# A chunked recurrence with a gated FFN: one mask tile for all heads, decay factors by a small DMA, and a new order of all steps

## The chip, the cores and the metric

The kernel runs on one core of one Trainium2 chip. The metric is device microseconds of one execution of the whole kernel. Three runs of the kernel before gave 170.5, 170.62 and 171.06; the median is 170.62. Such a core has a matrix engine (PE, which writes to eight PSUM banks), a vector engine (DVE), an activation engine (ACT), a general engine (POOL) and a sequencer (SP) that here only issues DMAs. Each engine works through its own list of instructions in order; they meet through semaphores.

## The reference

```python
# r, k, v, w: (4, 8, 768, 48) f32; u: (8, 48)
for t in range(S):
    kt, vt, rt, wt = (k[:, :, t], v[:, :, t], r[:, :, t], w[:, :, t])
    cur = np.einsum('bhd,bhe->bhde', u[None] * kt, vt)
    y[:, :, t] = np.einsum('bhd,bhde->bhe', rt, state + cur)
    state = wt[:, :, :, None] * state + np.einsum('bhd,bhe->bhde', kt, vt)
...
x = y.transpose(0, 2, 1, 3).reshape(3072, 384)
a = x @ w1          # w1, w2: 384 x 1024
b = x @ w2
h = a * b @ w3      # w3: 1024 x 1024
return h @ w_out    # w_out: 1024 x 384
```

A recurrence over 768 time steps (4 batch rows, 8 heads, 48 channels a head) feeds a gated feed-forward block over 3072 tokens.

## The kernel before, in words

**Units.** Time is cut into six chunks of 128 steps. A unit (`UNITS`, L14) is one chunk of one or two batch rows: units 0 and 1 are chunk 0 of batch rows 0 and 1 alone, unit 2 is chunk 0 of rows 2 and 3, and units 3 to 12 are chunks 1 to 5, two batch rows each. `unit(t)` (L383) defines the recurrence of a unit, `block(t)` (L672) its feed-forward part, `loads(t)` (L310) its loads. The inputs are f32 in HBM; most loads go through POOL's queue, which converts them to bf16 on the way.

**Inside a unit.** `ln` takes the logarithm of w (L402). `cs` sums it along time by a matmul with the triangular matrix `LT` (L414), and, in every unit but those of the last chunk, adds one matmul with one column of ones for each pair of heads (L419): that gives the sum over the whole chunk with channels on partitions. `pc` (L426) takes its exponential, the factor by which the state decays over the chunk. `ne` and `e` (or `et`) take exponentials of the running sums with a minus or plus sign, and k and r are scaled by them (`KRk` L438, `KRr` L484 or `KRw` L468). Both are transposed, on PE (`trk`, `trr`, `trw`, with a copy back, `trke`, `trre`) or, in later units, by a DMA that SP issues (`dtr`, `dtk`). Units in `RAW` transpose r unscaled and get the running sum transposed by `csT` (L451). `m` (L549) multiplies the transposes to scores M[s, t]; scores with s >= t are set to zero, either by DVE in one multiply with `mask` out of PSUM (`msk`, L568) or, for those in `POOL_MASK`, by a copy on ACT (`mcp`, L555) and a multiply on DVE (L561) or a select on POOL (L563). `rk`, `ruk`, `dg`, `dv` (L518 to L537) give the diagonal term with u. `ys` multiplies with the state, `yi` (L594) the scores with v; `yb` (L612) adds the diagonal (for unit 1, in `Y_PE`, two matmuls `yd` at L603 and a copy do). y is transposed (`yt` and `xT`, or a DMA `dty`). `kv` (L647), `T` (L655), `S` (L663, with pc) and `Sb` (L668) carry the state on.

**Feed-forward.** w3 and w_out are multiplied once: `wt` transposes w3 (L365), `w3Te` copies it back, `wm` (L374) multiplies with w_out and `w34e` copies. wm_0 is the first of these eight products. Then `a` and `b` (L688) multiply with w1 and w2, `asb` copies a to SBUF on ACT (L693), `abT` multiplies it by b on DVE (L698), `o` (L704) multiplies with the product of w3 and w_out, `osb` copies (L709) and `st` stores (L714).

**Order.** Nothing is scheduled by a compiler. `ORDER` (L61) lists every step with its engine (`dv_8@POOL`); each engine's program is what the list gives it, in that order. `warm7@3` stands for three matmuls on zeros into bank 7 (L302), whose result nobody reads. `BANKS` (L38) gives each step its PSUM bank or buffer, so a step also waits for the one that used the bank before.

The change touches the constants, `LT`, `mask` and `u` at the start (L206 to L298), `cs` and `pc`, the two places that use the mask, and both lists.

Of the kernel before, what the change touches and what calls it, by code (L numbers as in the profile page):

```python
# [7 lines left out]
F32 = mybir.dt.float32  # L8
# [12 lines left out]
N_M = 4  # L21
N_PC = 4
N_X = 4
N_ASB = 3
# [4 lines left out]
RAW = {0, 1, 2, 3, 6}  # L29
N_PSUM = set()  # L30
DMA_R = {7, 8, 9, 10, 11, 12}
# [29 lines left out]
ORDER = """  # L61
table@ACT zeros@DVE u@SP win_0@POOL kin_0@SP rin_0@SP win_1@POOL vin_0@SP rin_1@POOL win_3@POOL kc_0@DVE padlw@DVE
padet@DVE ones@DVE kin_1@POOL mask1@DVE LT@POOL win_2@POOL ln_0@ACT rc_0@DVE rk_0@DVE warm0@18 cs_0@PE padr@DVE
kin_2@POOL padkr@DVE ln_1@ACT uc@ACT warm1@6 csT_1@PE w3_0@POOL pc_0@ACT cs_1@PE ruk_0@DVE et_1@ACT ne_0@ACT
vin_1@POOL pc_1@ACT I128@POOL mask@POOL warm3@9 trw_1@PE csT_0@PE trw_0@PE ln_3@ACT kin_3@POOL ne_1@ACT warm4@3
csT_3@PE KRk_1@DVE KRk_0@DVE rin_3@POOL rk_1@DVE warm6@2 trk_0@PE vc_0@DVE trk_1@PE KRw_1@DVE trke_0@ACT dg_0@DVE
rin_2@POOL et_0@ACT et_3@ACT KRw_0@DVE ruk_1@DVE w3_1@POOL warm7@8 m_0_0@PE trke_1@DVE ln_2@ACT cs_3@PE msk_0_0@DVE
wo@POOL kv_0@PE cs_2@PE vin_3@POOL m_1_0@PE pc_2@ACT ne_2@ACT msk_1_0@DVE warm4@2 wt_0_0@PE w3_2@POOL pc_3@ACT
wt_1_0@PE ne_3@ACT wt_0_1@PE dg_1@DVE vin_2@POOL kv_1@PE csT_2@PE S_0@DVE dv_0@DVE yi_1_0@PE et_2@ACT dv_1@DVE
win_4@POOL S_1@DVE warm7@3 yd_1@PE KRk_3@DVE ybc_1@ACT KRk_2@DVE warm7@2 trk_3@PE w3Te_0@ACT win_5@POOL Sb_0@DVE  # L70
yt_1@PE yi_0_0@PE wt_1_1@PE Sb_1@ACT yb_0@DVE trw_3@PE w3Te_1@ACT trke_3@DVE w1_1@POOL warm1@1 trw_2@PE KRw_3@DVE
trk_2@PE KRw_2@DVE warm4@1 m_3_1@PE rk_3@DVE warm7@1 m_3_0@PE trke_2@DVE mcp_3_0@ACT rin_4@POOL ruk_3@DVE warm7@4
m_2_0@PE wt_2_0@PE maff_3_0@DVE mcp_2_0@ACT ys_3@PE wt_2_1@PE msk_3_1@DVE xT_1@ACT maff_2_0@POOL warm0@1 wt_3_0@PE
warm1@1 wt_3_1@PE dg_3@DVE m_2_1@PE yt_0@PE mcp_2_1@ACT rk_2@DVE kin_4@POOL warm4@3 wm_0@PE ruk_2@DVE maff_2_1@POOL
yi_3_0@PE w3Te_2@DVE wm_1@PE w34e_0@DVE dv_3@POOL dg_2@DVE yi_3_1@PE w3Te_3@ACT wm_2@PE rin_5@POOL yb_3@DVE w34e_1@ACT
wt_4_0@PE xT_0@DVE wt_5_0@PE w2_1@POOL wt_4_1@PE w3Te_4@DVE warm0@1 yi_2_0@PE wm_3@PE kin_5@POOL w34e_2@DVE dv_2@DVE
wt_5_1@PE yi_2_1@PE ln_4@ACT w1_0@POOL w34e_3@DVE yt_3@PE wm_4@PE yb_2@DVE w3Te_5@ACT xT_3@DVE iw_4@ACT cs_4@PE
w2_0@POOL w34e_4@DVE wm_5@PE pc_4@ACT ln_5@ACT ne_4@ACT cs_5@PE w3_3@POOL a_0_1@PE e_4@ACT yt_2@PE pc_5@ACT iw_5@ACT
rw_4@DVE kv_2@PE vin_4@POOL a_3_2@PE ne_5@ACT xT_2@DVE KRr_4@DVE a_1_1@PE asb_0_1@ACT S_2@DVE win_6@POOL kv_3@PE
asb_1_1@ACT KRk_4@DVE trr_4@PE T_3@DVE e_5@ACT a_2_2@PE rw_5@DVE win_7@POOL trre_4@ACT a_2_3@PE KRr_5@DVE trk_4@PE  # L80
S_3@DVE w34e_5@ACT trr_5@PE asb_2_3@ACT rk_4@DVE vin_5@POOL b_2_2@PE Sb_3@ACT ruk_4@DVE trre_5@DVE b_2_3@PE b_1_1@PE
KRk_5@DVE rin_7@POOL b_3_2@PE abT_1_1@DVE b_0_1@PE dg_4@DVE asb_2_2@ACT trk_5@PE kin_6@POOL abT_0_1@DVE a_1_0@PE
trke_5@ACT abT_2_2@DVE a_0_0@PE abT_2_3@DVE asb_1_0@ACT a_3_0@PE rin_6@POOL asb_0_0@ACT trke_4@DVE a_2_1@PE
asb_3_2@ACT b_0_0@PE abT_3_2@DVE asb_2_1@ACT m_4_0@PE abT_0_0@DVE m_4_1@PE mcp_4_0@ACT a_3_3@PE msk_4_1@DVE wt_6_0@PE
Sb_2@ACT b_1_0@PE asb_3_0@ACT maff_4_0@DVE wt_6_1@PE ys_4@PE abT_1_0@DVE dv_4@POOL m_5_0@PE yi_4_0@PE msk_5_0@DVE
b_2_1@PE asb_3_3@ACT wt_7_0@PE ln_6@ACT win_8@POOL yi_4_1@PE a_3_1@PE yb_4@DVE wt_7_1@PE win_9@POOL b_3_0@PE rk_5@DVE
w3Te_7@ACT cs_6@PE abT_2_1@DVE ln_7@ACT kin_7@POOL b_3_1@PE w3Te_6@DVE a_2_0@PE ruk_5@DVE iw_7@ACT abT_3_0@DVE wm_7@PE
pc_6@ACT asb_3_1@ACT dg_5@DVE ne_6@ACT abT_3_1@DVE csT_6@PE dv_5@POOL asb_2_0@ACT yt_4@PE et_6@ACT cs_7@PE xT_4@DVE
kv_4@PE rw_7@DVE rin_8@POOL pc_7@ACT kv_5@PE ne_7@ACT a_4_3@PE T_5@DVE rk_6@DVE wm_6@PE e_7@ACT kin_8@POOL KRk_6@DVE
asb_4_3@ACT T_4@DVE win_10@POOL KRr_7@DVE ys_5@PE m_5_1@PE ln_8@ACT S_4@DVE b_4_0@PE msk_5_1@DVE vin_6@POOL w34e_7@ACT  # L90
yi_5_0@PE trw_6@PE iw_8@ACT b_4_3@PE w34e_6@DVE vin_7@POOL Sb_4@ACT trk_6@PE KRw_6@DVE ln_9@ACT yi_5_1@PE abT_4_3@DVE
b_2_0@PE rin_10@POOL yb_5@DVE a_4_0@PE win_11@POOL cs_8@PE trke_6@DVE asb_4_0@ACT b_3_3@PE pc_8@ACT iw_9@ACT
abT_4_0@DVE vin_9@POOL a_4_2@PE KRk_7@DVE ne_8@ACT a_4_1@PE abT_3_3@DVE S_5@POOL e_8@ACT abT_2_0@DVE o_0_0@PE
ruk_6@DVE asb_4_2@ACT kin_9@POOL rk_7@DVE asb_4_1@ACT m_6_0@PE rw_8@DVE ln_10@ACT ys_6@PE rin_9@POOL m_6_1@PE
KRr_8@DVE o_2_0@PE mcp_6_1@ACT msk_6_0@DVE iw_10@ACT cs_9@PE dg_6@DVE yt_5@PE pc_9@ACT yi_6_0@PE xT_5@ACT o_3_0@PE
maff_6_1@DVE ruk_7@DVE ne_9@ACT osb_0_0@DVE yi_6_1@PE osb_2_0@ACT b_5_1@PE dv_6@DVE st_0_0@SP e_9@ACT st_2_0@SP
b_4_1@PE dtr_7@SP Sb_5@ACT yb_6@DVE a_5_1@PE ln_11@ACT a_5_2@PE dg_7@DVE dtr_8@SP asb_5_1@ACT yt_6@PE rk_8@DVE
# [36 lines left out]
def kernel(  # L134
# [629 lines left out]
```

## Time and profile before

| | us |
|---|---|
| three runs, median | 170.62 |
| the profiled execution | 171.16 |
| its span, first to last instruction | 169.4 |
| PE busy (1998 matmuls) | 162.6 |
| DVE busy (221 instructions) | 134.1 |
| ACT busy (151) | 89.5 |
| POOL busy (83) | 86.2 |

The profiled execution is 1.76 us longer than its span; that is what lies around it. Busy times are of engines that work side by side. A busy PE is not a PE that does useful work: matmuls on zeros count too. The chain of waits follows the work that ended last back to the start and names, at each step, what it stood on.

### The profile page before, as it was taken

The numbers are of one execution on the slowest core, as the hardware profiler recorded it, in microseconds if no ns is written. First come the engines' busy times: TensorE is split into PE (matmuls) and PEld (weight loads), VectorE is DVE, ScalarE is ACT, GpSimd is POOL, SyncE is SP. The second block draws the span as 40 slices with busy tenths as digits, with TensorE's granted clock in tenths as the row PEclk, the third lists the DMA queues.
The fourth block names the chain that finished last, engine by engine and source line by source line (L and its number), as shares of the span: only waits on it lengthen the run. The fifth ranks groups of instructions, "written<-read, shape, count | busy, mean of one in ns | idle before, by whom it ended". The sixth has DMA issues, their size and how long they took to land.

```text
span 169.4 us, 4733 instructions
## 1 busy us (share of the span) xinstructions
PE 162.6 (96%) x1998; PEld 122.0 (72%) x1998; DVE 134.1 (79%) x221; ACT 89.5 (53%) x151; POOL 86.2 (51%) x83
## 2 busy tenths in 40 slices
PE   7999999999999999999999999999999799999991
PEld 2455765676999887876878787676888587686860
DVE  0568889786789999999999999997799867556260
ACT  3166575258947789689855986611632042330511
POOL 7899874894773838994049607294072023000000
PEclk9999999999999999999999999999999999999999
DMA  3999999999999999999959999959949944603313
GB/s 80 212 205 182 146 198 189 206 215 153 183 203 217 175 173 167 172 149 174 194 106 90 174 203 236 164 49 109 135 109 141 157 87 109 165 4 95 137 58 130
DMA packets 98837, 25.63 MB, mean 151 GB/s; under 512 B 90880, under 2 KB 96640, under 8 KB 98816
## 3 DMA queue, kind: packets, MB, share of 16 engines
q0 software_dynamic: 76320, 15.96, 104.3%
q1 hardware_dynamic: 22496, 9.38, 27.3%
q8 instruction: 15, 0.25, 0.6%
q14 instruction: 6, 0.05, 0.1%
HBM read 27.98 MB, written 4.72 MB: 193 GB/s over the span
## 4 chain that ended last, share of the span: by engine, by line
PE 73%; DVE 11%; DMA 7%; ACT 4%; issue 2%; POOL 1%; SPq 0%; DVEq 0%; ACTq 0%
PE banks L688 28%; PE banks L704 13%; PE banks L302 10%; PE banks L374 6%; DMA vin<-in_v_dram 5%; PE banks L549 3%; DVE abT L698 3%; PE banks L594 2%; PE banks L414 2%; PE banks L510 2%; PE banks L365 1%; DMA out_dram<-osb 1%; DVE dg L528 1%; ACT a_sb L693 1%; PE banks L647 1%
## 5 line engine op out<-in xcount | busy, mean ns | idle before, releaser
L688 PE MATMUL banks<-xT,w_bf 128*128 128x256 bf16 (+1 forms) x624 | 69.7, 264 | 0.5 <-DMA xT<-yb 0.4
L688 PEld LDWEIGHTS <-w_bf 128*128 128x128 bf16 x624 | 55.2, 98 | 7.8 <-issue 1.0
L693 ACT COPY a_sb<-banks 128x512 f32<-128x512 f32 x48 | 27.4, 594 | 27.8 <-PE banks L688 22.5
L698 DVE TENSOR_TENSOR abT<-a_sb,banks 128x512 bf16<-128x512 f32 x48 | 31.6, 681 | 10.4 <-PE banks L688 6.9
L704 PE MATMUL banks<-w,abT 128*128 128x384 bf16 x192 | 34.5, 326 | 0.1
L704 PEld LDWEIGHTS <-abT 128*128 128x128 bf16 x192 | 18.1, 98 | 10.7
L568 DVE TENSOR_TENSOR Mbf<-banks,mask 128x1024 bf16<-128x1024 f32 x17 | 20.4, 1219 | 1.6 <-PE banks L549 1.3
L302 PE MATMUL banks<-zeros 128*128 128x512 bf16 x66 | 19.9, 431 | 1.4 <-DVE zeros L243 1.3
L537 POOL TENSOR_TENSOR dv<-vin,dg 128x768 bf16<-128x768 bf16 x9 | 13.3, 1482 | 15.5 <-DMA vin<-in_v_dram 8.7
L709 ACT COPY osb<-banks 128x384 f32<-128x384 f32 x13 | 6.3, 482 | 21.7 <-PE banks L704 9.2
L329 POOL DMA_DIRECT2D win<-in_w_dram x13 | 15.0, 1157 | 1.1 <-POOLq L748 0.8
L329 POOL DMA_DIRECT2D rin<-in_r_dram x12 | 13.8, 1152 | 2.8 <-DMA w_bf<-in_moe_w_dram 2.5
L402 ACT ACTIVATE lw<-win 128x768 bf16<-128x768 f32 (+1 forms) x13 | 10.5, 811 | 8.7 <-DMA win<-in_w_dram 8.7
L329 POOL DMA_DIRECT2D vin<-in_v_dram x12 | 13.9, 1160 | 2.3 <-DMA w_bf<-in_moe_w_dram 0.9
L329 POOL DMA_DIRECT2D kin<-in_k_dram x12 | 13.8, 1153 | 1.7 <-issue 0.7
L612 DVE TENSOR_TENSOR yb<-banks,dv 128x768 bf16<-128x768 f32 (+1 forms) x12 | 11.1, 921 | 4.4 <-issue 1.8
L302 PEld LDWEIGHTS <-zeros 128*128 128x128 bf16 x66 | 6.5, 108 | 8.2 <-issue 3.8
L433 ACT ACTIVATE NEt<-banks 128x768 bf16<-128x768 f32 (+1 forms) x13 | 9.9, 765 | 3.6 <-PE banks L414 3.6
L663 POOL TENSOR_TENSOR Sst<-Tst,pc 128x384 f32<-128x384 f32 x4 | 3.7, 934 | 15.7 <-DVE Tst L655 15.6
L374 PE MATMUL banks<-wo_bf,w3T 128*128 128x384 bf16 x64 | 11.7, 325 | 0.0
L528 DVE TENSOR_REDUCE dg<-ruk 128x16 f32<-128x768 bf16 (+1 forms) x13 | 11.5, 881 | 0.0
L594 PEld LDWEIGHTS <-Mbf 128*128 128x128 bf16 x192 | 7.8, 96 | 2.5 <-issue 1.1
(83 smaller groups left out, 222.5 us busy)
## 6 DMA issues: line engine op xcount, KB each, us to landing
out_dram<-osb SPq DMA_DIRECT2D x24, 192.0 KB, 2.1
win<-in_w_dram POOLq DMA_DIRECT2D x11, 384.0 KB, 9.8
kin<-in_k_dram POOLq DMA_DIRECT2D x11, 192.0 KB, 7.8
rin<-in_r_dram POOLq DMA_DIRECT2D x11, 192.0 KB, 8.4
vin<-in_v_dram POOLq DMA_DIRECT2D x11, 192.0 KB, 8.7
w_bf<-in_moe_w_dram POOLq DMA_DIRECT2D x4, 512.0 KB, 11.6
w_bf<-in_moe_w_dram POOLq DMA_DIRECT2D x4, 384.0 KB, 12.3
wo_bf<-in_moe_w_out_dram POOLq DMA_DIRECT2D x1, 768.0 KB, 13.5
```

Source lines behind the costliest of these rows:

```text
L302: nc.tensor.matmul(banks[:, at, :], lhsT=zeros[:, :C], rhs=zeros, start=True, stop=True)
L329: QUEUE[eng].dma_start(dst, src)
L374: nc.tensor.matmul(one(f"wm{fi}")[:, :DM], lhsT=w3T[fi % 2][:, gi, :], rhs=wo_bf[:, gi, :], start=(gi == 0), stop=(gi == FI - 1))
L528: nc.vector.reduce_sum(dgs, ruks, axis=AX.X)
L537: e.tensor_mul(dvs, vv, dgs[:, :, None].to_broadcast([C, bh, D]))
L568: nc.vector.tensor_mul(Mbf[bank[f"M{t}_{b}"]], mview(), mask.rearrange("s (j q) t -> s j q t", j=2))
L594: nc.tensor.matmul(o[:, h % 2, b, h // 2, :], lhsT=M[:, h % 2, h // 2, :], rhs=vv[:, b * H + h, :], start=(not c and b == 0 and h < 2), st ...
L612: nc.vector.tensor_add(ybs.rearrange("t b (q e d) -> t e (b q) d", e=2, d=D), yview().rearrange("t e (x d) -> t e x d", d=D), dvs.rearrang ...
L688: nc.tensor.matmul(o[:, f, :], lhsT=wt[:, di, fi * P:(fi + 1) * P], rhs=x[:, di, :T], start=(di == 0), stop=(di == DI - 1))
L693: copier(eng)(a_sb[bank[f"sa{t}_{g}"]], one(f"a{t}_{g}"))
L698: nc.vector.tensor_mul(ab[:, g * per:(g + 1) * per, :T], sa.rearrange("p (f t) -> p f t", t=T), one(f"b{t}_{g}").rearrange("p (f t) -> p f ...
L704: nc.tensor.matmul(one(f"o{t}_{b}")[:, :DM], lhsT=ab[:, fi, b * C:(b + 1) * C], rhs=w34[:, fi, :], start=(fi == 0), stop=(fi == FI - 1))
```

## The change

- `mask` is one 128x128 tile, made on DVE as LT minus the identity, and is read again for each head. Before it was 128 x 8 x 128, a memset on DVE and a select on POOL.
- For units 6 to 10 (`ROW_PC`) the one-column matmuls go. `px` (ACT) takes the exponential of the last 32 rows of the running sum, for each batch row, into a row buffer `prow` (one buffer); `pd` (SP) sends the last row, 4 KB, to the 128 partitions of `pc`. For the other units the one-column matmuls are a step of their own, `cc`, apart from `cs`.
- u is loaded as one row of 384 numbers and spread to all partitions by a matmul with the first row of LT (`ub`) and a copy (`ue`). Before, the DMA wrote it to 128 partitions.
- `u_f` and the f32 landing places of unit 0's k, r and v share memory with the last two `abT` buffers. `Mbf` has 5 buffers for 4, `a_sb` 4 for 3.
- Unit 0 is no longer in `RAW`, unit 1 no longer in `Y_PE`; `POOL_MASK` is another set.
- `ORDER` and `BANKS` are new throughout. The 66 matmuls on zeros become 30. The first loads are issued by SP (w of unit 0, u, k), ACT (w of unit 1, r and v of unit 0) and POOL (the rest). 46 steps change their engine, most of them from DVE to ACT. vin_12 stands ahead of S_9 on POOL, vin_11 behind S_10; before, both stood behind S_9 and ahead of S_10.

```diff
-N_M = 4
+N_M = 5
-N_ASB = 3
+N_ASB = 4
-RAW = {0, 1, 2, 3, 6}
+RAW = {1, 2, 3, 6}
+ROW_PC = {6, 7, 8, 9, 10}
-POOL_MASK = {(2, 0), (2, 1), (3, 0), (4, 0), (6, 1), (7, 1), (8, 1)}
-Y_PE = {1}
+POOL_MASK = {(1, 0), (2, 0), (2, 1), (4, 1), (5, 0), (6, 1), (7, 1), (9, 1)}
+Y_PE = set()
...
+    prow = many(1, [P, P * NB * HP], F32, "prow")
...
-    mask = sb.tile([C, 2 * HP, C], BF, name="mask")
+    mask = sb.tile([C, C], BF, name="mask")
...
-        nc.gpsimd.affine_select(mask, mask, compare_op=Alu.is_gt, fill=0.0, base=0, channel_multiplier=-1,
-                                pattern=[[0, 2 * HP], [1, C]])
+        nc.vector.tensor_sub(mask, LT, I128)
...
-        nc.sync.dma_start(u_f, u.rearrange("h d -> (h d)").partition_broadcast(C))
+        QUEUE[eng].dma_start(u_f, u.rearrange("h d -> (h d)").rearrange("(p x) -> p x", p=1))
...
+        nc.tensor.matmul(one("ub")[:, :DM], lhsT=LT[0:1, :], rhs=u_r, start=True, stop=True)
...
-            if state:
+        if state and t not in ROW_PC:
+            @op(f"cc_{t}")
+            def _(eng):
                 o = col_view()
...
+        if state and t in ROW_PC:
+            @op(f"px_{t}")
+            def _(eng):
+                dst = own(prow)[96:].rearrange("t (e d b q) -> t b q e d", e=2, b=nb, q=HP)
+                for b in range(nb):
+                    nc.scalar.activation(dst[:, b, :, :, :D], cs_view()[96:, b].rearrange("t (q e d) -> t q e d", e=2, d=D),
+                                         Act.Exp)
+            @op(f"pd_{t}")
+            def _(eng):
+                QUEUE[eng].dma_start(PC, own(prow)[C - 1:C])
...
-                        nc.vector.tensor_mul(x, x, mask)
+                        nc.vector.tensor_mul(x, x, mask[:, None, :].to_broadcast([C, 2 * HP, C]))
...
-                    nc.vector.tensor_mul(Mbf[bank[f"M{t}_{b}"]], mview(), mask.rearrange("s (j q) t -> s j q t", j=2))
+                    nc.vector.tensor_mul(Mbf[bank[f"M{t}_{b}"]], mview(),
+                                         mask[:, None, None, :].to_broadcast([C, 2, HP, C]))
```

More of the change, by code (lines that the diff above doesn't have):

```diff
@@ L63 @@
[L63 to L92, printed above, removed]
@@ L128 @@
-asb_12_1@ACT o_11_0@PE abT_12_1@DVE o_12_1@PE osb_11_0@DVE st_11_0@SP st_9_0@SP o_12_0@PE osb_12_1@DVE st_12_1@SP
-osb_12_0@ACT st_12_0@SP
+zeros@DVE win_1@ACT win_0@SP padlw@DVE ones@DVE rin_0@ACT u@SP LT@POOL table@ACT kin_0@SP padr@POOL vin_0@ACT
+kin_1@POOL win_3@POOL ln_0@ACT ln_1@ACT warm0@8 cs_0@PE rin_1@POOL uc@ACT e_0@ACT cc_0@PE kc_0@DVE cs_1@PE win_2@POOL
+ne_0@ACT iw_0@ACT padet@DVE rc_0@DVE cc_1@PE csT_1@PE pc_1@ACT ub@PE pc_0@ACT I128@POOL KRk_0@DVE ue@ACT vin_1@POOL
+padkr@DVE ne_1@ACT rw_0@DVE vc_0@ACT warm4@4 trk_0@PE KRr_0@DVE w3_0@POOL padpx@DVE trr_0@PE KRk_1@DVE mask@DVE
```

206 lines of the change are left out of this document (124 added, 82 removed).

## The prediction

> **What bounds the kernel now.** I read the page first, then the chain of waits in order of time, then the busy time by stage.
>
> ```profile
> span 169.4 us, 4733 instructions
> PE 162.6 (96%) x1998; PEld 122.0 (72%) x1998; DVE 134.1 (79%) x221; ACT 89.5 (53%) x151; POOL 86.2 (51%) x83
> DMA  3999999999999999999959999959949944603313
> ```
>
> PE is busy 96% of the span, and the DMA engines are full (nine tenths or more) in nearly every slice up to 100 us. But "busy" does not mean useful here. The chain shows what PE was doing:
>
> ```profile
> 1.26 6.93 PE banks L302 x18
> 8.52 1.32 PE banks L302 x6
> ...
> 17.40 0.18 PE banks L419 x8
> ...
> 30.48 0.65 PE banks L302 x3
> 31.13 1.30 PE banks L374 x8
> ...
> 36.10 0.22 PE banks L302
> ...
> 161.77 3.91 PE banks L704 x24
> ```
>
> L302 is the warm-up matmul on zeros: filler that computes nothing. There are 66 of them, 65 ahead of 31.13 us, where the first product of w3 and w_out (wm_0, L374) starts. After it there is one, at 36.10. So the kernel has two parts with different limits. Ahead of wm_0, PE is not the bound: it fills its waits. From wm_0 on, PE runs real work to 161.77 + 3.91 = 165.68, and after that only a copy and a store are left (169.4 - 165.68 = 3.7 us of tail).
>
> ```profile
> core 0: us, PE busy (x) PEld busy (x) DVE busy (x) ACT busy (x) POOL busy (x), PEclk, DMA share, GB/s
> 8.00:31.00 23.00, 22.77 (x287) 14.46 (x286) 19.27 (x41) 14.54 (x26) 18.62 (x20) 1.00 1.73 186
> 31.00:42.00 11.00, 11.00 (x122) 7.51 (x121) 7.85 (x14) 5.76 (x10) 8.49 (x9) 1.00 1.79 190
> 42.00:92.00 50.00, 50.00 (x748) 42.48 (x745) 47.23 (x77) 38.44 (x66) 31.78 (x28) 1.00 1.80 168
> 92.00:134.00 42.00, 41.81 (x545) 31.71 (x544) 38.96 (x58) 19.65 (x34) 18.25 (x16) 1.00 1.29 150
> 134.00:165.70 31.70, 30.33 (x292) 23.34 (x289) 18.42 (x27) 8.86 (x16) 2.95 (x2) 1.00 0.38 96
> ```
>
> From 31 us on PE is idle only 42.00 - 41.81 = 0.19 and 31.70 - 30.33 = 1.37, together 1.56 us. DVE is nearly full from 42 to 92 (47.23 of 50), so the chain passes through it there, but PE does not starve. What sets the start of wm_0 is a load:
>
> ```profile
> 16.72 0.94 POOL L348 DMA_DIRECT2D wo_bf<-in_moe_w_out_dram  x1
> wo_bf<-in_moe_w_out_dram POOLq DMA_DIRECT2D x1, 768.0 KB, 13.5
> u_f<-in_u_dram SPq DMA_DIRECT2D x1, 192.0 KB, 3.8
> ```
>
> w_out is issued at 16.72 and lands 13.5 us later, at 30.2. The other loads stand ahead of it in full DMA engines. So the time is: start of wm_0, plus PE's work after it, plus PE's idle time, plus the tail: 31.13 + (134.55 - 1.56 = 132.99) + 1.56 + 3.7 = 169.4.
>
> **The change part by part: the start of wm_0.** I compared the two orders. The same loads stand ahead of w_out in both (w, k, r of units 0 to 3, v of units 0 and 1, two quarters of w3), so its landing moves by bytes. u goes from 192 KB spread over 128 partitions to one row of 1.5 KB. At the stage's 186 GB/s the 195,000 bytes saved are 1.05 us: landing at about 29.15. The first loads now leave from SP, ACT and POOL at once instead of SP and POOL. The first DMA slice (4.2 us) is only three tenths busy, so an earlier flow could give up to about 0.9 us more, and I keep 28.3 as the lower end. The Trainium skill ("DMA: Bandwidth & Descriptors", section "Issuing engines are not separate DMA queues") says that starting DMAs from several engines saves only the issuing time; by it the landing would stay at 29.15, and the sum goes by that anyway.
>
> PE's own steps ahead of wm_0 are the same set in both orders but for unit 0: csT_0, trw_0, yd_1 go; trr_0 and the u matmul come. What DVE does there:
>
> ```profile
> L285 DVE MEMSET mask<- 128x1024 bf16 x1 | 0.9, 912 | 0.2 <-issue 0.2
> L514 DVE COPY KRT<-banks 128x1024 bf16<-128x1024 bf16 x4 | 2.7, 683 | 0.0
> L568 DVE TENSOR_TENSOR Mbf<-banks,mask 128x1024 bf16<-128x1024 f32 x17 | 20.4, 1219 | 1.6 <-PE banks L549 1.3
> L561 DVE TENSOR_TENSOR Mbf<-Mbf,mask 128x1024 bf16<-128x1024 bf16 x4 | 2.8, 704 | 0.1
> ```
>
> DVE loses the mask memset (0.91), two copies of transposes (2 x 0.68, to ACT) and a masked eviction (1.22, to ACT and POOL); it gets an eviction at 1.22 for a multiply at 0.70, and one multiply (0.70) that POOL did. yb_1, one w3T copy and unit 0's two new products stand against v's conversion, KRw_0 and padr, about even. In all some 2 us less, beside 19.27 of 23 us now, so I take the landing as the limit. In before, three warm-ups (0.65 us) stand directly ahead of wm_0 and it starts 0.9 after the landing; in the new order one stands there. So 29.15 + 0.4 = 29.55: **1.6 us earlier**. Bounds: 28.3, and 31.1 if DVE and ACT get through units 0 to 3 no sooner than now.
>
> **PE's work after wm_0.** The steps are again the same set. Out go the one-column matmuls of units 6 to 10, five groups of eight at 0.18 = **0.9 us**, and the warm-up at 36.10, **0.2 us**. Changes between 64-row and 128-row matmuls are as many as before (31). Left: 131.9.
>
> **What replaces the columns.** Each pc activation becomes two px activations of 384 elements on 32 partitions, and a 4 KB DMA that turns one partition's row into 128 partitions of 8 numbers. No row shows either. For px the ends are the pc row and the 384-element row; I take the upper, as the elements per partition are the same: 0.96 for 0.18, five times, 3.9 us more on ACT. For the DMA the ends are 2.6 (the fastest SP transfer) and 6.9 (an SP load behind two others at the full start); I take 3, as SP holds nothing else then.
>
> ```profile
> L426 ACT ACTIVATE pc<-banks 128x8 f32<-128x8 f32 x9 | 1.6, 180 | 1.7 <-PE banks L419 1.7
> L433 ACT ACTIVATE NEt<-banks 128x384 bf16<-128x384 f32 x2 | 1.0, 480 | 0.0
> wide_r<-in_r_dram SPq DMA_DIRECT2D x1, 192.0 KB, 6.9
> xT<-yb SPq DMA_TRANSPOSE x10, 2.6
> L709 ACT COPY osb<-banks 128x384 f32<-128x384 f32 x13 | 6.3, 482 | 21.7 <-PE banks L704 9.2
> L514 ACT COPY KRT<-banks 128x1024 bf16<-128x1024 bf16 x2 | 2.0, 1012 | 1.9 <-PE banks L510 1.9
> L693 ACT COPY a_sb<-banks 128x512 f32<-128x512 f32 x48 | 27.4, 594 | 27.8 <-PE banks L688 22.5
> ```
>
> The result is wanted late: between px_6 and S_6 PE has 25 us of work by these rates. The stretch of the order that PE now runs from 42 to 92 gives ACT 72 steps for 65: beside px three more osb (1.4), two more KRT copies (2.0), one more copy of scores, of the same size (1.0) and one more a_sb (0.6); the rest evens out. ACT gets 38.4 + 9 = 47.4 of 50 us. DVE has 76 steps for 78. Both fit, barely; ACT's cover is thin.
>
> **The mask** as one tile read again for each head: the nearest rows are ruk, which reads u again for each batch row, and rk, which reads nothing twice:
>
> ```profile
> L522 DVE TENSOR_TENSOR ruk<-rk,u_bc 128x768 bf16<-128x768 bf16 x11 | 6.1, 557 | 0.1
> L518 DVE TENSOR_TENSOR rk<-rin,kin 128x768 bf16<-128x768 bf16 x11 | 6.0, 549 | 0.0
> ```
>
> 8 ns apart: I count nothing. The other end would be the four SBUF multiplies at 1219 for 704, 2 us on DVE.
>
> **PE's idle time.** Of the 1.56 us, 0.9 is one wait:
>
> ```profile
> PE banks L594 <- DMA vin<-in_v_dram: 0.9, 1, 0.9
> 126.31 8.74 DMA vin<-in_v_dram
> 135.09 0.36 PE banks L594 x8
> ```
>
> POOL issues vin_12 and vin_11 behind S_9 (and vin_11 just ahead of S_10), and yi_11_0 wants vin_11 at once. In the new order vin_12 comes ahead of S_9, and between vin_11 and yi_11_0 PE has about 17 us of work, twice the 8.74: this wait goes. What is late next is unknown: every order was found anew, so I take 0.7 us of new idle, nearest to the 0.66 that the old order has beside vin. Net **0.2 us** less. Ends: no new idle, and the slower rival.
>
> **Sum:** 1.6 + 0.9 + 0.2 + 0.2 = 2.9 us off the span, 166.5. The profiled execution took 171.16 (span 169.4 and 1.76 around it), 0.54 over the median of 170.62; from the median, 167.7.
>
> **The rivals.** (1) *The start is not set by w_out.* If units 0 to 3 pass DVE and ACT no earlier, wm_0 stays at 31.1 and 1.3 us are left: 169.3. For it: DVE is 84% busy there. Against it: the load is later than all but one of these steps now.
>
> (2) *Slower: ACT waits for the small DMA.* prow is one buffer, so px of a unit waits until the DMA of the unit before has landed, and ACT's later steps (a_sb, which frees PE's banks) queue behind it. px_6, 7, 8 and 9 stand 4.6 to 4.9 us of PE work apart; less 0.96 for px, it costs from a landing of 3.7 us on. With 6.9, three waits of 3.2 = 9.6 us, at about 54 to 69 us, where the DMA row shows nine tenths; ACT's free 2.6 us of the stage take some, 7 us reach PE: 174.7. Against it: 4 KB on an otherwise empty SP queue.
>
> (3) *A cold array.* The first 18 warm-ups took 6.93 us, 0.385 each, the next six 0.22: PE starts at half rate. With 30 warm-ups for 66, PE ahead of wm_0 has long holes. If it is at half rate when wm_0 starts, the steps that end the prologue (some 1.5 us) double and wm starts slow for about as long as at the start (the early excess, 18 x (0.385 - 0.22) = 3 us): 4.5 in all, cut to about 3 because some of it hides behind w_out's landing: 170.7, no change. The Trainium skill ("TensorE: Matmul & The Clock Gate", section "Part 1: The HAM clock gate") says that the array falls back to half rate after an idle window of about 3.4 us; the two rates are in these rows, the falling back in none. Against it: the holes are broken by warm-ups and by units 0 to 3.
>
> (4) *The change doesn't do what it says*: the columns hide behind something. From 31 us PE is never idle for long, so this holds only where DVE sets the pace (73 to 92 us); units 8 and 9 then give nothing, 0.4 us: inside the forecast.
>
> **How the numbers follow.** Forecast 0.54, its own range 165.8 (wm_0 at 28.3, no new idle) to 169.0; rival 1 0.17; rival 2 0.18; rival 3 0.08; more gain than the bounds 0.03. A measurement of this kernel tells about 0.3% (0.5 us) from no change. Faster: 0.54 + 0.17 + 0.03, less 0.03 for rival 1 with more new idle time, is 0.71. Same: that 0.03 and 0.06 of rival 3, 0.09. Slower: rival 2 and the worse 0.02 of rival 3, 0.20. The range leaves out the lowest case and the upper half of rival 2: 165.3 to 171.8.
>
> **What would show it.** wm_0's first matmul at 29 to 30 us, right behind w_out's landing (rival 1: well behind it). No one-column matmuls for units 6 to 10, and PE's work from wm_0 to its last matmul near 131.9 plus idle. No wait of PE on vin. ACT's px near 0.48 each; the DMA's landing near 3 us, and no ACT wait on it (rival 2: a row of px waiting for that DMA). Warm-ups and transposes at half rate past 20 us would be rival 3. The forecast is wrong if PE's idle time after wm_0 exceeds 4 us, or w_out lands after 31.

## The result, and the profile after

| | before | changed |
|---|---|---|
| median of the runs of this comparison, us | 170.84 (4 runs) | 185.91 (4 runs) |
| the profiled execution | 171.16 | 184.54 |
| its span | 169.4 | 182.8 |

The ratio is 1.085, interval [1.077, 1.093]: the changed kernel is 8.5% slower; the forecast was 1.7% faster. Throughout, executions more than 1.5% above the fastest of their kernel do not enter the ratio (one of these four), the times given for e7, e9, e10, e16 and e17 are means of the executions that do, and the traces of e7, e16 and e17, which are of such long executions, are not read.

One correction to the section on the change: 48 steps change their engine, not 46, and 22 of them go from DVE to ACT.

The head of the page of the changed kernel; the DMA row is in 40 slices, 4.57 us each:

```profile
span 182.8 us, 4620 instructions
PE 160.6 (88%) x1917; PEld 119.4 (65%) x1917; DVE 127.9 (70%) x208; ACT 108.5 (59%) x186; POOL 84.1 (46%) x83
DMA  6999999999999999990069699977979901261213
```

PE is busy 88% of the span for 96%, ACT 108.5 us for 89.5. The first DMA slice is six tenths full for three. Around 82 to 91 us the DMA engines are empty, and then they fill again: the late loads come in a bunch. PE's instructions, in order of time, with the idle time ahead of them in brackets and what ended it (the first row, and those with the long waits):

```profile
27.80 2.44 PE L391 MATMUL banks<-wo_bf,w3T 128*128 128x384 bf16 x14
...
67.48 0.48 PE L434 MATMUL banks<-lw,LT 128*128 128x384 bf16 x2 [2.02 <-ACT lw L422]
...
80.52 1.91 PE L739 MATMUL banks<-w,abT 128*128 128x384 bf16 x7 [3.24 <-ACT NEt L467]
...
113.07 0.40 PE L583 MATMUL banks<-KRT 64*128 64x128 bf16 x8 [2.55 <-DMA KRT<-KR]
...
121.17 0.82 PE L723 MATMUL banks<-xT,w_bf 128*128 128x256 bf16 x6 [1.02 <-DVE yb L647]
...
129.22 1.47 PE L723 MATMUL banks<-xT,w_bf 128*128 128x256 bf16 x12 [2.14 <-DVE abT L733]
...
131.69 0.81 PE L723 MATMUL banks<-xT,w_bf 128*128 128x256 bf16 x6 [1.00 <-DMA xT<-yb]
```

wm_0 starts at 27.80. In the same view of the kernel before it starts at 30.97 (the 31.13 of the prediction is from the chain):

```profile
30.97 1.46 PE L374 MATMUL banks<-wo_bf,w3T 128*128 128x384 bf16 x8
```

So it comes 3.2 us earlier. The front gained, and more than forecast. The loss lies behind it, in two places. The busy time by stage, first of the changed kernel, then of the kernel before, shows both:

```profile
56.00:86.00 30.00, 22.68 (x300) 16.59 (x299) 22.59 (x33) 22.87 (x34) 16.17 (x14) 0.94 1.73 126
86.00:104.00 18.00, 17.90 (x216) 14.01 (x214) 16.11 (x28) 15.28 (x25) 8.09 (x6) 1.00 0.63 100
104.00:134.00 30.00, 23.24 (x337) 17.43 (x335) 19.62 (x31) 16.61 (x38) 12.14 (x11) 1.00 1.73 150
```

```profile
56.00:86.00 30.00, 30.00 (x464) 24.61 (x463) 29.35 (x46) 24.48 (x41) 18.42 (x16) 1.00 2.06 165
104.00:134.00 30.00, 29.98 (x399) 22.57 (x397) 27.08 (x39) 10.88 (x20) 13.04 (x11) 1.00 1.15 138
```

PE (the second number) idles 30.00 - 22.68 = 7.3 us from 56 to 86 us, where before it idled none, and 30.00 - 23.24 = 6.8 us from 104 to 134 us. Together 14.1. In the terms of the prediction's sum, wm_0 starts at 27.8, PE is then busy for 135.9 us and idle for 15.8 us until its last matmul ends at 179.5, and the tail is 3.3 us. In the first of these stages the granted clock (third from the end) is 0.94. It falls right behind the wait of 3.24 us, as the same view shows for 82 to 84 us:

```profile
82.00:84.00 2.00, 2.00 (x33) 1.18 (x33) 1.26 (x3) 1.88 (x4) 0.00 (x0) 0.50 0.00 0
```

So slow matmuls hide in the busy time too. The chain of waits names the first place:

```profile
14.13 0.91 POOL wo_bf L365
...
54.47 1.57 ACT prow L451 x2
...
56.07 6.49 DMA pc<-prow
...
62.65 1.58 ACT prow L451 x2
...
64.29 5.40 DMA pc<-prow
...
71.41 5.90 DMA pc<-prow
...
79.66 0.81 ACT NEt L467
...
80.52 2.23 PE banks L739 x8
```

This is rival 2 as the prediction drew it: px of a unit (`prow`, L451) waits until the small DMA of the unit before (`pc<-prow`) has landed, which takes 5.4 to 6.5 us, and the steps behind px on ACT (the logarithm L422, the exponential L467) reach PE late. The groups and the waits give the prices:

```profile
L451 ACT ACTIVATE prow<-banks 32x384 f32<-32x384 f32 x10 | 7.8, 883 | 5.6 <-DMA pc<-prow 5.5
L602 DVE TENSOR_TENSOR Mbf<-banks,mask 128x1024 bf16<-128x1024 f32 x16 | 19.2, 1220 | 3.0 <-PE banks L583 2.6
wo_bf<-in_moe_w_out_dram POOLq DMA_DIRECT2D x1, 768.0 KB, 13.3
DMA to landing us min/median/max: 2.1/5.4/6.5
```

A px activation takes 0.883 us, ten of them 7.8 us; ACT waits 5.5 us for the DMA. The last row is that of pd (issue to landing; smallest, median, largest of five). The first three took 6.5, 5.4 and 5.9 us. The fourth, issued at 78.96 as the last loads end, took 2.1 us; the DMA row falls to zero right behind it. The fifth, at 97.9 us, took 3.7.

### The profile page after: what moved, and what is told of

It is laid out like the page before. It is cut to its first block, busy times and chain, and to the rows that moved or that the text cites. A ratio compares the mean times of both kernels' runs of the same rounds, so it can differ in the third digit from the quotient of the medians.

```text
span 182.8 us, 4620 instructions
## 1 busy us (share of the span) xinstructions
PE 160.6 (88%) x1917; PEld 119.4 (65%) x1917; DVE 127.9 (70%) x208; ACT 108.5 (59%) x186; POOL 84.1 (46%) x83
## 4 chain that ended last, share of the span: by engine, by line
PE 44%; DMA 26%; POOL 9%; SPq 6%; ACT 6%; issue 4%; DVE 4%; DVEq 0%; ACTq 0%; POOLq 0%
PE banks L723 21%; PE banks L739 14%; DMA pc<-prow 10%; DMA vin<-in_v_dram 7%; DMA xT<-yb 4%; DMA KRT<-KR 4%; SPq L656 3%; ACT prow L451 3%; PE banks L583 2%; POOL win L346 2%; POOL rin L346 2%; DVE yb L647 2%; PE banks L391 2%; SPq L749 1%; PE banks L682 1%
## 5 line engine op out<-in xcount | busy, mean ns | idle before, releaser
L728 ACT COPY a_sb<-banks 128x512 f32<-128x512 f32 x48 | 27.8, 590 | 30.2 <-PE banks L723 24.6
L739 PE MATMUL banks<-w,abT 128*128 128x384 bf16 x192 | 35.2, 332 | 3.2 <-ACT NEt L467 3.2
L602 DVE TENSOR_TENSOR Mbf<-banks,mask 128x1024 bf16<-128x1024 f32 x16 | 19.2, 1220 | 3.0 <-PE banks L583 2.6
L744 ACT COPY osb<-banks 128x384 f32<-128x384 f32 x19 | 8.9, 482 | 17.8 <-PE banks L739 17.8
L571 POOL TENSOR_TENSOR dv<-vin,dg 128x768 bf16<-128x768 bf16 x8 | 12.0, 1504 | 15.6 <-issue 10.9
L346 POOL DMA_DIRECT2D win<-in_w_dram x11 | 13.0, 1180 | 0.3 <-issue 0.3
L422 ACT ACTIVATE lw<-win 128x768 bf16<-128x768 f32 (+1 forms) x13 | 10.4, 802 | 2.9 <-DMA win<-in_w_dram 2.9
L583 PE MATMUL banks<-KRT 64*128 64x128 bf16 x192 | 8.9, 225 | 3.6 <-DMA KRT<-KR 2.6
L319 PE MATMUL banks<-zeros 128*128 128x512 bf16 x30 | 10.9, 480 | 1.3 <-DVE zeros L251 1.3
L391 PE MATMUL banks<-wo_bf,w3T 128*128 128x384 bf16 x64 | 11.2, 326 | 0.1
L451 ACT ACTIVATE prow<-banks 32x384 f32<-32x384 f32 x10 | 7.8, 883 | 5.6 <-DMA pc<-prow 5.5
L467 ACT ACTIVATE NEt<-banks 128x768 bf16<-128x768 f32 (+1 forms) x13 | 10.0, 765 | 1.8 <-PE banks L434 1.3
L698 POOL TENSOR_TENSOR Sst<-Tst,pc 128x384 f32<-128x384 f32 x4 | 4.4, 1111 | 13.7 <-issue 12.0
## 6 DMA issues: line engine op xcount, KB each, us to landing
wo_bf<-in_moe_w_out_dram POOLq DMA_DIRECT2D x1, 768.0 KB, 13.3
```

The costliest lines, as they stand in the source:

```text
L346: QUEUE[eng].dma_start(dst, src)
L391: nc.tensor.matmul(one(f"wm{fi}")[:, :DM], lhsT=w3T[fi % 2][:, gi, :], rhs=wo_bf[:, gi, :], start=(gi == 0), stop=(gi == FI - 1))
L451: nc.scalar.activation(dst[:, b, :, :, :D], cs_view()[96:, b].rearrange("t (q e d) -> t q e d", e=2, d=D), Act.Exp)
L571: e.tensor_mul(dvs, vv, dgs[:, :, None].to_broadcast([C, bh, D]))
L583: nc.tensor.matmul(o[:, e, q, :], lhsT=KRTs[a:a + PAD, 0, b * HP + q, :], rhs=KRTs[a:a + PAD, 1, b * HP + q, :], start=True, stop=True)
L602: nc.vector.tensor_mul(Mbf[bank[f"M{t}_{b}"]], mview(), mask[:, None, None, :].to_broadcast([C, 2, HP, C]))
```

## The experiments

All ratios are against the kernel before on the same chips (171.17 to 171.29 us in these comparisons). Where a step of 1% is called 1.7 us, that is 1% of 171.2.

**The row and its DMA.** Theory W: the wait for the single buffer is the loss. Its rivals: X, the cost of px itself on ACT; O, the new order.

e1_three_rows: the row gets three buffers, so that no px waits.

```diff
+    prow = [prow[0]] + [abT[i].rearrange("p f t -> p (f t)").bitcast(F32) for i in (N_AB - 1, N_AB - 2)]
+    row_of = {6: 0, 7: 1, 8: 2, 9: 0, 10: 0}
```

> The changed kernel with three row buffers in place of one (two of them in the memory of abT buffers that are free then), so that no px waits for the DMA of the unit before; order and everything else as changed. Theory W (the wait of px for that DMA stops ACT, and the stalls after 100 us are its late consequence): PE's idle time goes both at 65 to 81 us and at 110 to 135 us, 166 to 169 us in all. Rival X (px's own 8 us on a full ACT is the cause, not the wait): above 178. Rival O (the new order of POOL's and SP's queues collides late by itself): the front is mended and the stalls at 110 to 135 stay, 173 to 178.

Measured 181.3 (180.21 to 182.75), ratio 1.060 [1.053, 1.067]. The wait on the row is gone, and 2.5% (4.4 us) came back. W is true and is less than a third of the loss; its 166 to 169 us did not come, and the time lies in rival X's band. The group of px, two waits of PE and the stage from 104 to 134 us of this kernel:

```profile
L453 ACT ACTIVATE prow<-banks 32x384 f32<-32x384 f32 x6 | 4.7, 893 | 0.1
```

```profile
PE banks L725 <- DMA xT<-yb: 4.9, 3, 3.8
PE banks L585 <- DMA KRT<-KR: 3.0, 1, 3.0
```

```profile
104.00:134.00 30.00, 22.55 (x268) 15.92 (x269) 16.57 (x24) 12.15 (x31) 6.08 (x5) 0.83 1.26 121
```

(Six of the ten px write the first buffer and stand in this row.) PE now waits longer than in the changed kernel for transposing DMAs near 104 and 122 us, and the granted clock of the stage is 0.83.

e8_row_written_flat: px writes its 384 numbers side by side in eight runs of 48, not one every 32 bytes. The decay factors of units 6 to 10 then land on the wrong channels; everything else is as in e1.

> The three-rows kernel (181.3 us) with px writing its 384 results next to each other, not one every 32 bytes; pads and the small DMA read the same bytes, so the decay factors of units 6 to 10 land on wrong channels. Theory S (px takes 0.88 for 384 elements because of the spread write): 0.48 each, 4 us less on ACT, 177 to 180. Rival: px is slow for another reason (32 partitions, or the kind of function): 0.88 stays, 180 to 183.

Measured 178.92, ratio 1.040 [1.033, 1.047], 2.0% (3.5 us) less than e1. px:

```profile
L453 ACT ACTIVATE prow<-banks 32x384 f32<-32x384 f32 x6 | 2.6, 476 | 0.7 <-PE banks L436 0.7
```

0.893 has become 0.476: the same elements from the same PSUM cost 0.41 us less when they are written side by side. Ten of them are 4.1 us of ACT, of which 3.5 reached the end.

e2_columns_back: the changed kernel with the one-column matmuls in place of the row.

```diff
-ROW_PC = {6, 7, 8, 9, 10}
+ROW_PC = set()
...
-cs_6@PE ... px_6@ACT pd_6@SP
+cs_6@PE cc_6@PE ... pc_6@ACT
```

> The changed kernel with the one-column matmuls back for units 6 to 10 (a small pc activation at px's place, the columns right behind cs, no px, no DMA, no row buffer). Theories W and X both: 167 to 169 us, with 0.9 us of columns more than without. Rival O: 173 to 178, with PE still idle between 110 and 135 us. W and X part here only against the run with three rows: W says the two are within 1 us, X says this one is over 8 us faster.

Measured 176.12, ratio 1.030 [1.024, 1.035]: against e1 another 3.0% (5.2 us), between what W (1 us) and X (8 us) gave. So the row costs 4.4 us by its wait and 5.2 by its own time, mostly the spread write; and 3% are left that have nothing to do with it.

e3_row_in_old_order and e4_three_rows_old_order: the kernel before with px and pd for units 6 to 10, with one buffer and with three.

> The kernel before, with only px and the small DMA put in for pc of units 6 to 10, one row buffer, old order. pc of these units stood 2.6, 7.7, 6.0 and 10.7 us apart; px to px takes about 8 with the DMA (1.6 for px, 0.5 to issue, 5.9 to land). Theory W: ACT waits 5.4 + 0.3 + 2.0 = 7.7 us, of which its idle time takes a part: 173 to 177. Rival X: 8 us more on ACT with some idle time there: 171 to 174, and the same with three buffers. Rival O: 170 to 171, since the old order is kept.

> The same as the row in the old order, but with three row buffers, so that no px waits for a DMA. Theory W: 169.5 to 171 (0.9 us of columns less on PE, some of it lost to px's time on ACT). Rival X: no better than with one buffer. Rival O: as with one buffer, 170 to 171.

Measured 178.95, ratio 1.046 [1.044, 1.049], and 175.97, ratio 1.030 [1.028, 1.032]. Both are slower than any of the three theories gave. In the old order too the wait costs 1.6% (2.8 us) and the row without it 3.0% (5 us). The row is a loss in either order, even though it takes the column matmuls off PE.

**The rest of the new order.** e2 has no row and is still 5 us behind, although its wm_0 starts at 28.4. Its chain from 107 us on:

```profile
107.70 2.07 ACT dv L568 x9
...
109.96 1.46 ACT dv L568 x6
...
111.44 0.04 DVE yb L647
...
116.69 4.38 DMA xT<-yb
...
121.21 4.15 PE banks L723 x18
```

and its busy time around that wait (PE is the second number, the granted clock the third from the end):

```profile
116.00:118.00 2.00, 2.00 (x17) 1.49 (x16) 1.91 (x4) 0.51 (x2) 2.00 (x3) 1.00 0.52 148
118.00:121.00 3.00, 0.37 (x3) 0.00 (x0) 2.39 (x5) 0.48 (x1) 0.63 (x1) 0.90 1.81 119
121.00:127.00 6.00, 5.79 (x66) 3.99 (x68) 0.97 (x2) 1.76 (x3) 0.00 (x0) 0.50 1.11 151
```

PE waits for the transpose of y and then runs 6 us at clock 0.50. Two edits were tried on what stands ahead of the wait.

e5_diag8_on_pool: the sixteen multiplies of dv_8 (3.5 us on ACT, above) as one on POOL, `-dv_8@ACT +dv_8@POOL`.

> The columns-back kernel (176.1 us) with one step moved: the diagonal product of unit 8 from ACT (16 small multiplies, 3.7 us in a row there) to POOL, at the same place of the order. Theory D (that block on ACT delays yb of units 8 and 9, their transposing DMAs and so PE's 3 us wait at 118 us, which the half-rate clock behind it, granted 0.5 from 120 to 127 us, doubles): 170 to 173. Theory P (POOL's late loads collide with the transposing DMAs): 174 to 176.

Measured 175.81, ratio 1.028 [1.023, 1.033]: no difference from e2. As an account of the time, theory D fell. Its mechanism is there in part: in e5's trace PE waits 1.4 us for a transposed y instead of 2.8, and the granted clock stays at 1.00 from 118 to 130 us. But PE then waits 2.1 us for DVE's masked scores and 2.2 us for its abT, and nothing is won.

e6_loads_ahead: seven late loads (vin_8, win_12, vin_9, vin_10, kin_10, kin_11, rin_12) right behind rin_11 on POOL, where the DMA engines are empty.

> The columns-back kernel with POOL's seven last early loads (v of units 8 to 10, w of 12, k of 10 and 11, r of 12) moved ahead of the state, diagonal and mask steps of units 6 and 7 that held them up to 98 us, into the time around 80 us where the DMA engines are four tenths busy. Theory P: the transposing DMA that took 6.6 us at 98 takes some 2, the waits at 103 and 118 us shrink, 170 to 173. Theory D: the wait at 103 goes (1 us), the one at 118 stays, 174 to 176.

Measured 180.5, ratio 1.053 [1.047, 1.059]: worse by 2.3% (4 us). One wait of PE shows how:

```profile
PE banks L583 <- DMA KRT<-KR: 3.7, 1, 3.7
```

The loads now meet the transposes of k and r at 92 us. e7_both_moves, both edits together:

> Both moves together. Theories D and P each need only their own, so this is no faster than the better of the two by more than 1 us if one is the whole cause; if each holds a part, 168 to 171, near what the start of wm_0 at 28.4, 133 us of work, 1.5 of idle and the tail give (166.6 of span, 168.3).

179.9, ratio 1.051 [1.042, 1.060]: no better than e6 alone, so the two do not add up. And e12_unblock_pool_new, which starts from e5 and moves ln_12, kin_10 and vin_9 so that POOL does not wait for ACT with loads queued behind it:

> The new order with columns back and unit 8's diagonal product on POOL (175.8 us), and three steps moved: the logarithm of unit 12 on ACT (it waits for a late load and holds the score copy of unit 7 that POOL waits for) back to just ahead of its use, and the loads of k of unit 10 and v of unit 9 ahead of that POOL step. Theory L (late loads, held by POOL's steps, make DVE and then PE wait at 108 us): that wait of 2.3 us goes and some of what follows, 172 to 174. Rival (the moved loads meet the transposing DMAs, as with all seven moved): 176 to 180.

181.42, ratio 1.062 [1.058, 1.066], 3.4% more than e5. Its rival named the right kind of loss and too little of it:

```profile
PE banks L583 <- DMA KRT<-KR: 5.2, 2, 4.5
PE banks L723 <- DMA xT<-yb: 3.9, 1, 3.9
```

Both traces of loads brought forward (e6 and e12) show a longer wait for a transposing DMA. So the next edit asks only that loads keep clear of the transposes, whether they come earlier or later for it.

e13_two_loads_away: in e2, the two loads that fly beside the transposes of y are taken from there: kin_12 goes forward, vin_12 back.

```diff
-Sb_8@ACT vin_12@POOL b_7_1@PE ... kin_12@POOL
+rin_12@POOL kin_12@POOL ... vin_11@POOL vin_12@POOL
```

> The second kernel (new order, columns in place of the row) with two late loads of POOL moved away from the transposes of y: kin_12 right behind rin_12 (issued near 104 us instead of 117), vin_12 behind vin_11 (near 134 us instead of 116). In the second kernel y's transposing DMA, issued at 116.69, took 4.38 us beside these two, PE waited 2.84 us for it at 118.4 to 121.2, and the matmuls behind it ran at half clock to 128 us. Theory C (the collision of loads and transposes is the cause, the half clock its price): that DMA takes under 2 us, PE waits under 0.7 us, no half clock at 121 to 128; 2.5 + 3 us less than 176.1, so 170.5 to 172. Theory H (the wait is set by something else, such as the multiplies of ACT ahead of y; only the half clock is large): wait of 1.5 us or more stays, 174 to 176. Theory M (the loss only moves, since kin_12 now stands behind five loads and vin_12 comes late for the last product with v): a new wait of PE of 1.5 us or more for one of the two loads, or for a transposed k, 175 or more.

Measured 172.48 (172.06 to 173.0), ratio 1.007 [1.005, 1.010]: 2.3% (3.9 us) less than e2, from two lines of an order. PE's waits from 104 to 122 us in this kernel are these three:

```profile
109.15 0.37 PE L629 MATMUL banks<-vin,Mbf 128*128 128x48 bf16 x8 [1.13 <-DVE Mbf L602]
109.75 0.37 PE L629 MATMUL banks<-vin,Mbf 128*128 128x48 bf16 x8 [0.23 <-DVE Mbf L595]
...
118.07 2.12 PE L723 MATMUL banks<-xT,w_bf 128*128 128x256 bf16 x18 [1.08 <-DVE abT L733]
```

None is for a transpose, and the same 18 matmuls start 3.1 us sooner and take 2.12 us for 4.15. The transposing DMAs of y issued at 115.6 and 116.9 land after 2.3 and 2.4 us; those issued at 116.7 and 117.9 in e2 took 4.4 and 5.9. A part of the collision has only moved, as theory M feared: the transposes of y issued at 129.7 and 131.0, right behind the two loads of v, take 4.2 to 5.3 us, and PE waits 0.8 us for one of them.

e14_fillers_at_the_wait: e2 with eleven matmuls on zeros ahead of the wait, `+warm5@11` in front of a_8_2. The wait stays; only the array is kept busy.

> The second kernel (new order, columns in place of the row) with eleven matmuls on zeros, 0.22 us each, ahead of the matmuls with w1 at which PE waited 2.84 us for a transposed y. Nothing else moves. Theory H (an idle of nearly 3 us puts the array to half clock for the 7 us behind it): granted clock 1.0 through 121 to 128 us, the 18 matmuls behind the wait in about 2 us for 4.15, and 3 us less than 176.1: 172.5 to 174. Theory G (half clock in that stretch hides behind DVE and ACT, which set the pace anyway): the 18 matmuls are fast but the end moves by less than 1 us: 175 to 176.2. Rival: fillers overrun the wait and add to it, up to 1 us more than 176.1.

Measured 174.39, ratio 1.021 [1.015, 1.027]: 0.8% (1.4 us) less than e2.

```profile
118.00:121.00 3.00, 2.51 (x18) 1.53 (x16) 0.85 (x2) 0.99 (x2) 0.00 (x0) 1.00 2.22 150
121.00:127.00 6.00, 5.21 (x94) 4.15 (x95) 3.92 (x6) 0.77 (x2) 0.00 (x0) 1.00 0.76 160
```

The granted clock is 1.00 where it was 0.50. So the half clock is real and is gone with the fillers, but it is the smaller part: some 1.4 of the 3.9 us that go when the transpose is not held up at all. The intervals of this ratio and of e2's overlap, so 1.4 us is a rough size; the forecast of 3 us was too high.

e16_two_loads_away_in_changed: the same two moves in the changed kernel itself.

> The changed kernel as it is (row buffer and small DMA), with kin_12 right behind rin_12 and vin_12 behind vin_11. The changed kernel lost 5 to 7 us between 104 and 134 us beside the 9 us at the row buffer. Theory C: its waits at 126.8 and 130.4 us (2.1 and 1.0) and the slow clock behind them go, 185.9 less 3 to 5: 181 to 183. Theory M: PE waits for other transposes near 110 us anyway (2.55 us there), 184 to 187. The 9 us of the row buffer stay by both.

Measured 180.4 (mean of two), ratio 1.053 [1.044, 1.062], 3.2% less than the changed kernel's 1.085 in its own comparison. By the time alone, the collision was there too. The slow clock that this expectation counts on is not in the changed kernel's trace, whose granted clock is 1.00 from 104 to 134 us.

**The front.** e9_new_front_old_rest: the new order up to wm_0, the old one behind it, columns kept.

> Every step of the new order ahead of the first product of w3 and w_out (wm_0), then the remaining steps in the old order with their old engines and banks (two banks changed to fit), the one-column matmuls for all units, no row buffer. It takes the part of the change that the prediction put at 1.6 us and the traces at 2.6 to 3.3, without the rest. If that gain lasts: 167.5 to 169 us. Rival (it is given back: PE comes to the loads of w1 and w2 or to DVE's full stretch so much sooner, and waits there): 170 to 171.5.

Measured 172.9, ratio 1.010 [1.008, 1.012]; wm_0 starts at 27.9, and still nothing is won, less even than the rival gave. The two first waits of PE behind it:

```profile
31.62 0.36 PE L629 MATMUL banks<-vin,Mbf 128*128 128x48 bf16 x8 [2.31 <-DMA vin<-in_v_dram]
...
34.39 1.46 PE L391 MATMUL banks<-wo_bf,w3T 128*128 128x384 bf16 x8 [0.90 <-ACT w3T L386]
```

2.31 + 0.90 is the 3.1 us gained. A later wait of 1.41 us, for a copy on ACT at 148.9 us, is new as well; what brought it was not traced. e15_v3_earlier moves vin_3 ahead of win_4 on POOL:

> The kernel with the new front and the old rest, with vin_3 moved ahead of win_4 on POOL. There PE waited 2.3 us for vin_3 at 29.0 us, and 1.0 us for a copy of w3 on ACT at 33.3. vin_3 now lands about 2 us earlier, at 29.4 to 30. Theory Q (the front's gain was given back at that one wait): 1.5 to 2 us less than 173.2: 171.2 to 172, level with before. Rival R: the copy on ACT and the later waits take it back (1 us at 33, 1.4 us at 147), 172.5 to 173.3.

Measured 172.12, ratio 1.005 [1.003, 1.008]: 0.8 us less than e9, where 1.5 to 2 was expected. The next load is late in its turn, and the waits of this stretch come to 2.4 us for 3.2:

```profile
29.75 0.36 PE L629 MATMUL banks<-vin,Mbf 128*128 128x48 bf16 x8 [0.50 <-DMA vin<-in_v_dram]
...
32.51 1.46 PE L391 MATMUL banks<-wo_bf,w3T 128*128 128x384 bf16 x8 [0.90 <-ACT w3T L386]
...
34.93 0.84 PE L382 MATMUL banks<-I,w_bf 128*128 128x128 bf16 x12 [0.96 <-DMA w_bf<-in_moe_w_dram]
```

So in these two kernels the loads behind w_out did not come earlier because PE did.

e10_and_v_loads_ahead (e9) and e11_v_loads_ahead_old (the kernel before) move vin_12 and vin_11 behind kin_11, so that the 0.9 us wait for vin_11, the change's other aim in the prediction, goes:

> The same, with the loads of v of units 12 and 11 moved on POOL from behind the state step S_9 to behind the load of k of unit 11. If the wait of 0.9 us on v goes, 0.9 less than without; if the loads meet the transposing DMAs of units 8 to 10 (1.7 us to land with no load beside them, 4 to 5 with two or more), nothing or a loss.

> The kernel before with only those two v loads moved as there. Wait gone: 170.0 to 170.4; met by transposing DMAs: 171 to 173.

173.6, ratio 1.014 [1.013, 1.016], and 173.25 (171.98 to 174.47), ratio 1.012 [1.007, 1.017]. In the trace of the second the wait for v is gone, and this one has come:

```profile
PE banks L688 <- DMA xT<-yb: 2.8, 2, 2.4
```

The kernel before pays 0.9 us for v and by that keeps the transposes of y clear.

**What is left of e13.** e17_k10_first moves kin_10 ahead of vin_9.

> The kernel with the two loads moved away (172.48), with one more step moved on POOL: kin_10 ahead of vin_9 and vin_10, all three behind the same select on POOL. In that kernel DVE waited 1.83 us for kin_10 at 105.6 to 107.4, PE 1.13 us for DVE at 108 and 1.08 us at 117. Theory K (the late load of k is what is left of the loss at this place): kin_10 lands about 2 us earlier, DVE's wait goes, PE's two waits shrink to under 0.5 us together: 170.8 to 171.6, level with the kernel before. Rival: v of unit 9 is late in its place, or the sixteen multiplies on ACT set the pace: 172 to 173.

Measured 172.0, ratio 1.005 [1.002, 1.007]: e13 within the error. e18_k10_and_T4 also moves T_4 ahead of dg_5:

> The kernel above, and on DVE the step T_4 ahead of dg_5: at 58.4 PE waited 0.77 us for T_4, which stood behind a product that took 1.9 us and a sum of 0.95 us. If PE's waits add up, 0.7 us less than the kernel above: 170.1 to 170.9, at or just below the kernel before. Rival: the diagonal of unit 5 comes as much later and its wait takes the place, no difference.

175.04, ratio 1.021 [1.018, 1.025]. The move went one step too far: in the list T_4 now stands ahead of kv_4 too, the matmuls whose product it adds. In the trace T_4 runs at 57.74 us and kv_4 at 58.34, after PE has waited 1.85 us for T_4. So T_4 adds what the bank held before, the state is wrong from there on, and the time says nothing about the idea. No version beat the kernel before; e13, e15 and e17 come within 0.5 to 0.7%.

## Why the prediction was wrong, point by point

The runs split the 8.5% like this, in the order in which the parts were taken out: the wait for the single row 2.5%, the row itself 3.0%, the two loads beside y's transposes 2.3% (each with an error of 0.6 to 1.1%), and 0.7% left. In that 0.7% the front's gain is already counted: in e13's trace wm_0 starts at 28.33, 2.6 us earlier than before, but from there PE idles 4.7 us for 1.6 and is busy 0.8 us longer. The parts are not independent: in the changed kernel the two loads were worth 3.2%.

*The start of wm_0: 1.6 us forecast, 3.2 measured.* The direction was right; the size was outside the bounds that I gave (28.3 at the earliest). I moved the landing by bytes alone. It came by the issue as well: w_out leaves POOL at 14.13 for 16.72 and takes 13.3 us for 13.5, so it lands at 27.4. POOL's rows show why, since POOL is busy nearly all the time up to that issue in both kernels: two loads of w, 1.97 us of issuing, went to SP and ACT, the mask's select, 1.08 us, is gone, and so is a wait of 0.73 us; against that, POOL's first issue comes 1.35 us later. I had counted the extra queues only as a bound and the select's place on POOL not at all. But an earlier start only counts if what PE wants next is earlier too, and the prediction's sum assumed it. e9 shows that it is not.

*The columns: right, but "Left: 131.9" is not.* Their matmuls are out for units 6 to 10. They were worth 0.9 us of PE by their rate; the row that took their place cost 4.4 + 5.2 us. PE's busy time on the page is down because 36 matmuls on zeros are out as well; from wm_0 on it is 135.9 us. The spell at half clock from 81 to 85 us makes some 1.7 of the 4.0 us more; the rest is not explained.

*px at 0.48: wrong, 0.88.* The failed step is "I take the upper, as the elements per partition are the same". Element count set the price only while the write was dense: e8 has 0.476, within 1% of the row I took. The diff showed the write pattern (`t (e d b q)`, one number every 32 bytes). The Trainium skill ("Advanced Engine Details and Errata", section "SBUF Cachelines") says that an access pattern that goes to another 16-byte line with each element pays a penalty, and gives no size; e8 against e1 agrees, with a factor of 1.9. The ten px took 7.8 us where the forecast had 4.8; the 3.0 more would have made ACT's 47.4 of 50 us 50.4, more than the stage holds.

*The small DMA at 3 us: wrong, 5.4 to 6.5.* The failed step is "as SP holds nothing else then". The queue was empty, but the engines behind it were not: the DMA row of before shows nine tenths there, and I quoted it. The same four kilobytes took 2.1 us as the loads ended and 6.5 at the worst. The prediction's own other end, 6.9 from an SP load behind two others, was the nearer row for a transfer beside loads, and I took the nearest by the state of the queue.

*So rival 2 was the case, and 0.18 too little.* Its mechanism, its place (54 to 69 us forecast; ACT's px came late at 62.65, 69.77 and 77.40) and about its price came out: 7 us of idle PE forecast, 7.3 measured from 56 to 86 us, not all of it by this wait. That the two agree is partly luck: the 7 came from three waits of 3.2 us, 9.6 in all, less ACT's free time, and ACT's three waits were 2.23, 0.79 and 2.49, 5.5 in all. At the end the wait was worth 4.4 us (e1). Its "against", 4 KB on an empty queue, was the weak sentence.

*The mask: right.* 1220 ns with the mask read again for each head, 1219 before.

*New idle time 0.7 us: wrong by far, 6.8 from 104 to 134 us alone.* The failed step is "every order was found anew, so I take 0.7". I looked at what the move of vin_12 and vin_11 frees (the wait for vin did go) and not at what it then flies beside. e11 shows the price in the old order, e13 that of vin_12 and kin_12 in the new one. A chance for this kind of loss was in none of my rivals.

*Rival 3, the cold array: right in mechanism, wrong in place.* PE was not cold at wm_0. In e2 and e13 the clock did fall to 0.50 at 12 to 14 us, ahead of wm_0, but it was back at 1.00 from 16 us on. What cost time was mid-kernel, behind waits of 3.24 us (the changed kernel) and 2.84 us (e2): the clock fell to 0.50 for some 3.5 us in the first and 6 in the second. The Trainium skill ("TensorE: Matmul & The Clock Gate", section "Why this matters for your kernels") warns of idle gaps over about 3 us between bursts; e2's gap of 2.84 was enough here. e14 put the price at some 1.4 us of the end. The prediction gave the sign that would prove it wrong, "PE's idle time after wm_0 exceeds 4 us"; it was 15.8.

Left open: what causes the last 0.7% of e13. Several waits of PE of 0.4 to 1.1 us make up its idle time, and e17, which aimed at two of them, moved nothing that can be measured.

## What to carry to other kernels

Price a DMA by how full the DMA engines are when it flies, not by its size or by its queue, and a write by its pattern, not by its element count. When loads move, list the latency-bound transfers (transposes, small copies) that will fly beside them: here loads brought forward to cure waits of one to three microseconds made others of 2.4 to 4.5 (e6, e11, e12). Here an earlier start of the main stage was worth nothing while the loads that this stage wants next were not earlier too.

## What the runs showed of the hardware that was not expected

- An ACT activation that writes 384 f32 numbers, one every 32 bytes, takes 0.88 to 0.89 us; the same written in runs of 48 takes 0.476.
- A 4 KB DMA from SP landed 2.1 us after its issue began as the last loads ended, and 5.4 to 6.5 the three times that POOL's loads filled the DMA engines (56 to 77 us); a fifth, at 97.9 us with two loads in flight, took 3.7. A transposing DMA of y took 2.3 us at best and 5.9 at worst in e2, from issue to landing (smallest and largest; the middle is the median):

```profile
DMA to landing us min/median/max: 2.3/2.4/5.9
```

- An idle time of PE of 2.84 us (e2) was followed by 6 us at half clock, and one of 2.37 us (e11) by a granted clock of 0.76 from 120 to 125 us; with matmuls on zeros in the gap the clock stayed at 1.00.
